# Probabilities for the memory rows: turned on 64 columns and copied into blocks, and fill that does not stop at a tile's end

## The chip, the cores and the metric

The kernel runs on one NeuronCore of a Trainium2 chip. The metric is the time of one execution on the device, in microseconds (us). An execution that was profiled gives, besides its time, a record of every instruction on every engine: TensorE (PE, and PEld for its weight loads), VectorE (DVE), ScalarE (ACT), GpSimd (POOL) and SyncE (SP, which issues most of the DMA transfers). In all profile lines here, Lnnn is line nnn of the kernel before.

## The reference

A layer norm, an attention with a recurrent memory, a residual, a second layer norm and a feed-forward block, on 2048 tokens of 640 numbers. The attention has 32 heads of 128. It goes through the tokens in 64 segments of 32, and 8 memory rows are put in front of each segment:

```python
for s in range(n_seg):
    h = concatenate([mem, x[s]])            # 8 + 32 rows
    q, k, v = h @ Wq, h @ Wk, h @ Wv        # 32 heads x 128
    p = softmax(where(mask, q @ k.T * scale, -1e9))   # memory rows see all 40, tokens are causal
    o = (p @ v) @ Wo
    mem = o[:8]                             # memory of the next segment
    out[s] = o[8:]
h = x + out
y = h + relu(layernorm(h) @ w1 + b1) ** 2 @ w2 + b2
```

The memory rows make it a chain: the projections of segment s + 1 need the eight output rows of segment s.

## The kernel before, in words

**Steps.** `step(b, sp)` does one segment; 16 blocks b of 128 tokens have four segments each, 64 steps in all. Weights stay in SBUF. A step projects q, k and v of 32 rows: the 8 memory rows and the segment's first 24 tokens. The last 8 tokens of each segment ("tails") need no memory, so their projections are done for many segments at once, as fill. Each projection has two halves n = 0, 1 of 16 heads: five chunks of the model dimension times four column groups, 20 matmuls of 512 columns.

**The memory rows' softmax** is done ahead of the tokens', in two halves of 16 heads. `scores(n)` (L494) makes a tile sm in which partition 32g + 8j + m holds memory row m of the head numbered 4g + j in that half, over 40 keys. `soft1(n)` (L500 to L505) takes the maximum mx on DVE and the exponential em with its sum zm on ACT. `soft2a(n)` (L510 to L519) takes 1/zm into rm (L512), spreads the 8 tail keys into four blocks of 8 columns with the 0/1 mask `same` (L514), and makes pm (L516): the 64 columns of em, four times over, each copy times rm and times `own`, a 128x4 mask that is 1 for the g-th copy in the partitions of group g alone. `soft3` (L523) turns pm, 128x256, in blocks of 32x32 on DVE. The result pT holds, for group g, the turned probabilities of that group in its own 32 partitions and zeros in the others; so that one matmul per head group can take v's 128 partitions against it (`values(n)`, L526 to L537: 16 matmuls L531 and 4 L536). `values_out(n)` copies the result into oT, half 0 on ACT (L245), half 1 on DVE (L243).

**The order around it** is written by hand; each engine runs its instructions in the order of the program, and waits are added where data or buffers need them. After the second half of k the order on PE is: `scores(0)`, v's first half (px, L233; out by ACT L589), the first chunk of v's second half, `scores(1)`, the rest of v's second half (ps; out by ACT L609), the tokens' own scores (L581, tile sk), fill, `values(0)`, fill, `values(1)`, then the 64 matmuls with wo (pw, L269). On DVE: mx(0), kT, rm(0), L514, pm(0), mx(1), the first half's turn, rm(1), L514, pm(1), the second half's turn, the causal mask (L611), oT, and the tokens' softmax (L640 to L651). Behind wo come the rest of the fill and `token_values` of the step before, while ACT (L284, L285) and DVE (L286, L379) bring the eight new memory rows into hT, on which the next step's q projection waits. POOL spreads q into qz (L440, L442), copies tails into qT and kT (L388, L384) and scales the tokens' probabilities (L653, L656).

**Fill** is a list of units, each one chunk of a tail projection (4 matmuls) or a tenth of a tail's wo (4 or 8 matmuls of 320 columns), of which `portion` gives some 8 to a step. `run(q, n, held, stop)` runs n of them. The unit that ends a tile returns its evacuation; this is put into `held` and done by `settle` later, behind `values(1)`, or for wo behind the tokens' tk. With `stop` true, `run` ends there:

```python
            ahead = 0 if ready else max(1, len(fill) // 2)
            run(fill, ahead // 2, held, True)
            values(0, pT0, po[1][0])
            values_out(0, po[1][0])
            run(fill, ahead - ahead // 2, held, True)
            values(1, pT1, po[1][1])
```

**Buffers.** The PSUM pool `mm` has three tiles for the halves of q, k and v, for sk and for the fill. em has one buffer for both halves; pT had two. pm shares a buffer with the tokens' pk.

Of the kernel before, what the change touches and what calls it, by code (L numbers as in the profile page):

```python
# [9 lines left out]
ALU = mybir.AluOpType  # L10
AX = mybir.AxisListType
F32 = mybir.dt.float32
BF16 = mybir.dt.bfloat16
# [3 lines left out]
def kernel(  # L17
# [31 lines left out]
    TL = SEG - HD  # L49
# [12 lines left out]
    const = ctx.enter_context(tc.tile_pool(name="const", bufs=1))  # L62
# [6 lines left out]
    s1 = ctx.enter_context(tc.tile_pool(name="s1", bufs=1))  # L69
    s2 = ctx.enter_context(tc.tile_pool(name="s2", bufs=2))  # L70
# [20 lines left out]
    for g in range(G):  # L91
        r = slice(32 * g, 32 * g + 32)
        nc.vector.tensor_copy(out=same[r], in_=ident[r, r].rearrange("p (j k) -> p j k", k=TL))
    nc.vector.tensor_reduce(out=diag[:], in_=same[:], op=ALU.add, axis=AX.X)
    nc.vector.tensor_copy(out=same[:], in_=diag[:].unsqueeze(2).to_broadcast([128, 4, TL]))
    own = const.tile([128, G], BF16)
    qT = const.tile([128, H, SEG], BF16)
    CW = 5 * SEG
    hTs = [const.tile([128, DC * CW], BF16, name="hT%d" % k) for k in range(2)]
# [40 lines left out]
    for q in range(4):  # L140
        nc.vector.tensor_copy(out=o0[32 * q:32 * q + 32, :].rearrange("m (c f) -> m c f", f=32),
                              in_=mem0[:].rearrange("m (c q f) -> m q c f", q=4, f=32)[:, q])
# [92 lines left out]
    def mmtile():  # L235
        return mm.tile([128, 512], F32, tag="mm", name="ps")
# [54 lines left out]
    fill, late, mid, nook = [], [], [], []  # L291

    def run(q, n, held=None, stop=False):
        while n > 0 and q:
            out = q.pop(0)()
            if out and held is not None:
                held.append(out)
                if stop:
                    break
            elif out:  # L300
                out[1]()
            n -= 1
# [148 lines left out]
    def step(b, sp, v=None):  # L451
        s = b * 4 + sp
        last = s == NS - 1
        lhs = rows_of(b, sp)
        ready = v is not None
# [31 lines left out]
        sms, ems, zms = {}, {}, {}  # L487

        def scores(n):
            sm = chn.tile([128, 512], F32, tag="ch", name="sm")  # L490
            for j in range(4):
                for g in range(G):
                    p = n * 16 + g * 4 + j
                    nc.tensor.matmul(sm[32 * g:32 * g + 32, 0:NK], lhsT=qz[:, p, :], rhs=kT[:, p, :],  # L494
                                     start=(j == 0), stop=(j == 3), skip_group_check=True)
            sms[n] = sm

        def soft1(n):
            mx = s2.tile([128, 1], F32, tag="mx", name="mx")
            nc.vector.tensor_reduce(out=mx[:], in_=sms[n][:, 0:NK], op=ALU.max, axis=AX.X, negate=True)  # L500
            em = s2.tile([128, SEG + NK], BF16, tag="em", name="em", bufs=1)
            zm = s2.tile([128, 1], F32, tag="zm", name="zm")
            nc.scalar.activation(out=em[:, SEG:], in_=sms[n][:, 0:NK], func=ACT.Exp, bias=mx[:, 0:1], scale=1.0,  # L503
                                 accum_out=zm[:])
            ems[n], zms[n] = em, zm  # L505

        def soft2(n):
            return soft3(soft2a(n))

        def soft2a(n):  # L510
            rm = s2.tile([128, 1], F32, tag="rm", name="rm")
            nc.vector.reciprocal(out=rm[:], in_=zms[n][:])  # L512
            pm = s1.tile([128, HG, 32], BF16, tag="pk", name="pm")[:].rearrange("p (g a) k -> p g (a k)", g=G)
            nc.vector.tensor_tensor(out=ems[n][:, 0:SEG].rearrange("p (j k) -> p j k", k=TL),  # L514
                                    in0=ems[n][:, 2 * SEG:].unsqueeze(1).to_broadcast([128, 4, TL]), in1=same[:], op=ALU.mult)
            nc.vector.scalar_tensor_tensor(out=pm, in0=ems[n][:, 0:2 * SEG].unsqueeze(1).to_broadcast([128, G, 2 * SEG]),  # L516
                                           scalar=rm[:, 0:1], in1=own[:].unsqueeze(2).to_broadcast([128, G, 2 * SEG]),
                                           op0=ALU.mult, op1=ALU.mult)
            return pm  # L519

        def soft3(pm):
            pT = s2.tile([128, G, 2 * SEG], BF16, tag="pTm", name="pTm")
            nc.vector.transpose(out=pT[:], in_=pm)  # L523
            return pT

        def values(n, pT, po):  # L526
            cols = po[:, 0, 0:128]
            for j in range(4):
                i = n * 4 + j
                for k in range(4):  # L530
                    nc.tensor.matmul(cols[32 * k:32 * k + 32].rearrange("p (g i m) -> p i g m", g=G, i=4)[:, j],  # L531
                                     lhsT=v[:, i * E + 32 * k:i * E + 32 * k + 32],
                                     rhs=pT[:, :, SEG + j * M:SEG + (j + 1) * M],
                                     start=(j == 0), stop=False, skip_group_check=True)
            for k in range(4):
                nc.tensor.matmul(cols[32 * k:32 * k + 32].rearrange("p (g a) -> p g a", g=G), lhsT=vt4[:, sp, n, 32 * k:32 * k + 32], rhs=pT[:, :, 0:SEG],  # L536
                                 start=False, stop=True, skip_group_check=True)  # L537

        def values_out(n, po):
# [23 lines left out]
        vt4 = vt4s[b]  # L563
# [13 lines left out]
        def token_scores(n):  # L577
            skv = view()
            for j in range(4):
                for g in range(G):  # L580
                    nc.tensor.matmul(skv[32 * g:32 * g + 32, n * 4 + j, :], lhsT=qT[:, n * 16 + g * 4 + j, :],  # L581
                                     rhs=kT[:, n * 16 + g * 4 + j, :], start=True, stop=True,
                                     skip_group_check=True)
# [6 lines left out]
            ps1 = mmtile()  # L590
            proj(wv, "half", lhs, 1, ps1, 0, 1)
        if not last:
            pm0 = soft2a(0)
            scores(1)
            soft1(1)
            pT0 = soft3(pm0)
# [6 lines left out]
        if not last:  # L603
            sk = mmtile()
            token_scores(0)
            token_scores(1)
            pT1 = soft2(1)
        if not ready:
            nc.scalar.copy(out=v[:, 512:1024], in_=ps1[:])  # L609
        def causal(skv):  # L610
            nc.vector.tensor_tensor(out=skv[:, :, M:NK], in0=skv[:, :, M:NK],  # L611
                                    in1=mask[:].unsqueeze(1).to_broadcast([128, HG, SEG]), op=ALU.add)

        held = []
# [4 lines left out]
        po = po_tiles()  # L619
        if last:  # L620
            run(fill, max(1, (len(fill) - 3) // 2), held, True)
            token_values(s - 1, *prevs[-2], po)
            token_out(s - 1, po)
            settle(held, True)
            run(fill, 2, held)
            settle(held, True)
            causal(skv)
        else:
            ahead = 0 if ready else max(1, len(fill) // 2)
            run(fill, ahead // 2, held, True)  # L630
            values(0, pT0, po[1][0])
            values_out(0, po[1][0])
            run(fill, ahead - ahead // 2, held, True)
            values(1, pT1, po[1][1])
            causal(skv)
            values_out(1, po[1][1])
            settle(held, True)
# [14 lines left out]
        pkt = s1.tile([128, HG, TL], BF16, tag="pkt", name="pkt")  # L652
        nc.gpsimd.tensor_tensor(out=pkt[:], in0=ek[:, :, SEG:NK], in1=rk[:].unsqueeze(2).to_broadcast([128, HG, TL]),  # L653
                                op=ALU.mult)
        pk = s1.tile([128, HG, 32], BF16, tag="pk", name="pk")
# [3 lines left out]
        if not last:  # L659
# [10 lines left out]
            held = []  # L670
# [10 lines left out]
        pTt = s1.tile([128, 2, 32], BF16, tag="pTt", name="pTt")  # L681
# [105 lines left out]
    def start():  # L787
# [45 lines left out]
        for n in range(2):  # L833
# [31 lines left out]
    nc.gpsimd.memset(mask[0:TL], 0.0)  # L865
    nc.gpsimd.affine_select(out=mask[0:TL], in_=mask[0:TL], compare_op=ALU.is_ge, fill=NEG, base=HD,
                            pattern=[[-1, SEG]], channel_multiplier=1)
    nc.gpsimd.memset(own[:], 0.0)
    for g in range(G):
        nc.gpsimd.memset(own[32 * g:32 * g + 32, g:g + 1], 1.0)  # L870
# [4 lines left out]
    for b in range(2, NB):  # L875
        for which in "qk":
            u = tail_units(b, which)
            plan += [(4 * b - 3 + (which == "k"), 4 * b - 5, u[DC * n:DC * n + DC]) for n in range(2)]
    for b in range(10, NB):
        u = tail_units(b, "v")  # L880
# [81 lines left out]
    for t in range(S // NT):  # L962
# [8 lines left out]
        for fc in range(FC):  # L971
            ps = mmtile()
            for c in range(DC):
# [43 lines left out]
        for q in range(NK4):  # L1017
# [6 lines left out]
            for hh in range(2):  # L1024
                k = pr + 2 * hh
# [44 lines left out]
```

## Time and profile before

| | us |
|---|---|
| runs of the kernel | 966.51, 966.9, 968.98; median 966.9 |
| the profiled execution | 965.13 |
| its span, first to last instruction | 963.0 |
| PE busy | 930.4 (97%) |
| DVE, ACT, POOL busy | 711.7, 538.5, 280.7 |
| steps 1 to 62, each | 12.2 |
| L516, pm, 126 times | 61.1, 485 ns each |
| L523, the turn of pm, 126 times | 56.0, 445 ns each |
| granted clock of TensorE | 0.998 |

Busy time of PE counts an instruction from start to end, and matmuls overlap in it. The chain of waits follows the work that ended last back from step to step: what stands in it had nothing to hide behind, and what does not stand in it was beside other work. In the timeline a row is a start, a duration, the engine, the line, the operation, the tiles and the shapes, and how often.

### The profile page before, as it was taken

The page shows a single profiled execution, that of the slowest core. Times are in us where ns is not written, and L with a number is a line of the kernel's source. Part 1 is how long each engine was busy: PE and PEld are TensorE (multiplying, and loading weights), DVE is VectorE, ACT ScalarE, POOL GpSimd, SP SyncE. Part 2 cuts the span into 40 slices and gives each one's busy share as a digit, 9 for nine tenths or more (in the row PEclk, how much of TensorE's full clock was granted, in tenths as well). Part 3 has the DMA queues.
Part 4 walks back from the last instruction along what each step waited for, and adds up shares of the span by engine and source line. Part 5 has one row for each costly group of instructions (what it writes and reads, how often), then busy time and mean ns, then how long its engine had stood idle before and what let it go on. Part 6 is the DMA issues. An engine that isn't in the chain of part 4 may idle for free.

```text
span 963.0 us, 55579 instructions
## 1 busy us (share of the span) xinstructions
PE 930.4 (97%) x24749; PEld 556.5 (58%) x24760; DVE 711.7 (74%) x2068; ACT 538.5 (56%) x1397; POOL 280.7 (29%) x875
## 2 busy tenths in 40 slices
PE   6979999999999999999999999999999999999998
PEld 2445566556565656556565656556655565555555
DVE  5178888778877787887878787878887788656532
ACT  2546666566666566666666566656665665523321
POOL 2113323232323222322232223232323233254300
PEclk9999999999999999999999999999999999999999
DMA  9972201010101001110101010101010220543320
GB/s 354 402 254 69 39 17 28 14 29 14 23 19 27 17 18 27 20 25 9 32 14 31 12 32 12 33 13 33 6 34 6 54 42 21 190 119 82 97 55 28
DMA packets 65872, 56.63 MB, mean 59 GB/s; under 512 B 37384, under 2 KB 61712, under 8 KB 63712
## 3 DMA queue, kind: packets, MB, share of 16 engines
q1 hardware_dynamic: 65392, 52.74, 19.3%
q8 instruction: 194, 3.18, 1.4%
q14 instruction: 46, 0.38, 0.1%
q0 software_dynamic: 224, 0.33, 0.1%
q10 hardware_dynamic: 16, 0.01, 0.0%
HBM read 38.37 MB, written 9.44 MB: 50 GB/s over the span
## 4 chain that ended last, share of the span: by engine, by line
PE 70%; DVE 17%; ACT 5%; DMA 4%; issue 2%; SPq 2%; ACTq 0%; POOL 0%; DVEq 0%
PE ps L233 19%; PE pw L269 15%; PE px L233 9%; PE pk L233 7%; PE y L1027 6%; PE ps L975 6%; DVE pm L516 5%; DVE kT L484 4%; DVE pTm L523 2%; PE ps L269 2%; ACT em L503 2%; DMA wq<-in_A_Wq_dram 2%; PE po L420 2%; PE po L531 2%; SPq L150 2%
## 5 line engine op out<-in xcount | busy, mean ns | idle before, releaser
L233 PEld LDWEIGHTS <-hT 128*32 128x32 bf16 x7680 | 190.8, 96 | 175.0 <-DVE hT L379 15.8
L269 PE MATMUL pw<-wo,oT 128*32 128x320 bf16 x4224 | 159.7, 299 | 4.3 <-issue 1.9
L269 PEld LDWEIGHTS <-oT 128*32 128x32 bf16 x4224 | 119.7, 96 | 26.7 <-issue 7.8
L257 DVE STREAM_TRANSPOSE qT<-row 128x512 bf16<-128x512 bf16 x128 | 89.5, 699 | 42.7 <-ACT row L252 42.5
L653 POOL TENSOR_TENSOR pkt<-ek,rk 128x64 bf16<-128x64 bf16 x64 | 18.9, 295 | 286.1 <-ACT otmp L285 213.7
L233 PE MATMUL ps<-wv,hT 128*32 128x512 bf16 x1260 | 89.5, 378 | 0.0
L647 ACT ACTIVATE ek<-tk 128x320 bf16<-128x320 f32 x64 | 30.1, 470 | 100.6 <-DVE tk L642 99.5
L233 PE MATMUL ps<-wq,hT 128*32 128x512 bf16 x1260 | 81.2, 382 | 3.2 <-DVE hT L379 3.0
L233 PE MATMUL ps<-wk,hT 128*32 128x512 bf16 x1280 | 80.5, 379 | 0.0
L233 PE MATMUL px<-wq,hT 128*32 128x512 bf16 x1260 | 79.4, 379 | 0.0
L233 PE MATMUL px<-wv,hT 128*32 128x512 bf16 x1260 | 79.2, 378 | 0.0
L233 PE MATMUL pk<-wk,hT 128*32 128x512 bf16 x1240 | 78.2, 379 | 0.0
L431 ACT CAST oT<-po 128x512 bf16<-128x512 f32 x128 | 68.7, 589 | 15.1 <-PE po L425 12.5
L983 ACT ACTIVATE wv<-ps,b1f 128x512 bf16<-128x512 f32 (+1 forms) x56 | 37.6, 672 | 66.6 <-PE ps L975 65.6
L233 PEld LDWEIGHTS <-hTt 128*32 128x32 bf16 x1920 | 53.1, 97 | 29.6 <-issue 4.7
L440 POOL COPY qz<-qT 128x96 bf16<-128x96 bf16 x126 | 33.4, 265 | 109.5 <-DVE qT L257 109.5
L516 DVE SCALAR_TENSOR_TENSOR pm<-em,rm,own 128x256 bf16<-128x256 bf16 x126 | 61.1, 485 | 4.6
L284 ACT COPY otmp<-pw 64x96 f32<-64x96 f32 (+2 forms) x129 | 28.9, 224 | 58.0 <-PE pw L269 36.9
L1027 PE MATMUL y<-wq,wk 128*128 128x320 bf16 x416 | 58.9, 299 | 0.2
L252 ACT ACTIVATE row<-ps 128x512 bf16<-128x512 f32 x93 | 54.7, 611 | 5.5 <-PE ps L233 4.7
L523 DVE STREAM_TRANSPOSE pTm<-pm 128x256 bf16<-128x256 bf16 x126 | 56.0, 445 | 2.2
L481 ACT CAST row<-ps 128x256 bf16<-128x256 f32 x126 | 40.8, 375 | 29.6 <-PE ps L233 29.6
(132 smaller groups left out, 1801.4 us busy)
## 6 DMA issues: line engine op xcount, KB each, us to landing
wv<-in_A_Wv_dram SPq DMA_DIRECT2D x5, 1024.0 KB
wq<-in_A_Wq_dram SPq DMA_DIRECT2D x5, 1024.0 KB
wk<-in_A_Wk_dram SPq DMA_DIRECT2D x5, 1024.0 KB
wo<-in_A_Wo_dram SPq DMA_DIRECT2D x8, 640.0 KB
o_all<-o SPq DMA_DIRECT2D x256, 7.5 KB
vt<-vt_d SPq DMA_DIRECT2D x60, 64.0 KB
xt<-in_A_x_dram SPq DMA_DIRECT2D x19, 160.0 KB
wq<-in_B_w_dram SPq DMA_DIRECT2D x1, 2080.0 KB
```

What stands on the lines that cost most here:

```text
L233: nc.tensor.matmul(ps[32 * k:32 * k + 32, :], lhsT=lhs(c), rhs=wr[:, c, n, k], start=(c == 0), stop=(c == DC - 1))
L252: nc.scalar.mul(out=row, in_=ps, mul=scale)
L257: nc.vector.transpose(out=dst[:, n * 16:(n + 1) * 16, 0:32], in_=row.rearrange("p (h e) -> p h e", e=32))
L269: nc.tensor.matmul(pw[32 * j:32 * j + 32, c0:c0 + DH], lhsT=lhs(p), rhs=wov2[:, head(p), ch], start=(h == 0), stop=(h == 15))
L431: nc.scalar.copy(out=oTg[:, gs, :, :, 0:SEG], in_=po[1][h][:, :, 0:256].rearrange("p g (n j q) -> p g n j q", n=2, q=32))
L481: nc.scalar.copy(out=row[:, u * 256:(u + 1) * 256], in_=ps[:, u * 256:(u + 1) * 256])
L484: nc.vector.transpose(out=dst[:, n * 16 + u * 8:n * 16 + u * 8 + 8, 0:32], in_=row[:, u * 256:(u + 1) * 256].rearrange("p (h e) -> p h e", ...
L516: nc.vector.scalar_tensor_tensor(out=pm, in0=ems[n][:, 0:2 * SEG].unsqueeze(1).to_broadcast([128, G, 2 * SEG]), scalar=rm[:, 0:1], in1=own ...
L523: nc.vector.transpose(out=pT[:], in_=pm)
L975: nc.tensor.matmul(ps[:], lhsT=w1[:, c, fc * 128:(fc + 1) * 128], rhs=hnT[:, c, :], start=(c == 0), stop=(c == DC - 1))
L983: nc.scalar.activation(out=r[:, 0:w], in_=ps[:, 0:w], func=ACT.Relu, bias=b1f[:, fc:fc + 1], scale=1.0)
L1027: nc.tensor.matmul(y[hh][:, 0:DH], lhsT=f1T[:, fc, k * 128:(k + 1) * 128], rhs=w2[:, fc, cs], start=(fc == 0 and not hf), stop=(fc == FFUL ...
```

## The change

For the first half of the heads the probabilities are no longer spread over 256 columns before the turn. `soft2(0)` multiplies em's 64 columns by rm into a 128x64 pm (in the buffer of the tokens' pkt). `soft3` turns these 64 columns (into the buffer of the tokens' pTt) and copies the four groups of 32 partitions, 32x64 each, into their blocks of a constant tile pBs[0]: group 0 on DVE, 1 on ACT, 2 and 3 on POOL. The rest of pBs[0] is set to zero once, on POOL, at the start. The second half is made as before, in pBs[1], which has one buffer now. ACT's copy of v's second half (L609) stands ahead of `soft2(1)` in the program; ACT's and DVE's own orders are not changed by that. For the fill, `ahead` is rounded up and `stop` is no longer given, so that a run goes on into the next tile when one ends; the evacuations still wait in `held`.

```diff
+    pBs = [const.tile([128, G, 2 * SEG], BF16, name="pB%d" % k) for k in range(2)]
...
         def soft2(n):
-            return soft3(soft2a(n))
-
-        def soft2a(n):
             rm = s2.tile([128, 1], F32, tag="rm", name="rm")
             nc.vector.reciprocal(out=rm[:], in_=zms[n][:])
-            pm = s1.tile([128, HG, 32], BF16, tag="pk", name="pm")[:].rearrange("p (g a) k -> p g (a k)", g=G)
             nc.vector.tensor_tensor(out=ems[n][:, 0:SEG].rearrange("p (j k) -> p j k", k=TL),
                                     in0=ems[n][:, 2 * SEG:].unsqueeze(1).to_broadcast([128, 4, TL]), in1=same[:], op=ALU.mult)
+            if n == 0:
+                pm = s1.tile([128, HG, TL], BF16, tag="pkt", name="pm")[:].rearrange("p i k -> p (i k)")
+                nc.vector.tensor_scalar(out=pm, in0=ems[n][:, 0:2 * SEG], scalar1=rm[:, 0:1], scalar2=None, op0=ALU.mult)
+                return pm
+            pm = s1.tile([128, HG, 32], BF16, tag="pk", name="pm")[:].rearrange("p (g a) k -> p g (a k)", g=G)
             nc.vector.scalar_tensor_tensor(out=pm, in0=ems[n][:, 0:2 * SEG].unsqueeze(1).to_broadcast([128, G, 2 * SEG]),
                                            scalar=rm[:, 0:1], in1=own[:].unsqueeze(2).to_broadcast([128, G, 2 * SEG]),
                                            op0=ALU.mult, op1=ALU.mult)
-            return pm
+            nc.vector.transpose(out=pBs[1][:], in_=pm)
+            return pBs[1]
 
         def soft3(pm):
-            pT = s2.tile([128, G, 2 * SEG], BF16, tag="pTm", name="pTm")
-            nc.vector.transpose(out=pT[:], in_=pm)
-            return pT
+            pT = s1.tile([128, 2, 32], BF16, tag="pTt", name="pT")[:].rearrange("p u k -> p (u k)")
+            nc.vector.transpose(out=pT, in_=pm)
+            for g, copy in enumerate((nc.vector.tensor_copy, nc.scalar.copy, nc.gpsimd.tensor_copy, nc.gpsimd.tensor_copy)):
+                r = slice(32 * g, 32 * g + 32)
+                copy(out=pBs[0][r, g], in_=pT[r])
+            return pBs[0]
...
-            pT1 = soft2(1)
         if not ready:
             nc.scalar.copy(out=v[:, 512:1024], in_=ps1[:])
+        if not last:
+            pT1 = soft2(1)
...
-            ahead = 0 if ready else max(1, len(fill) // 2)
-            run(fill, ahead // 2, held, True)
+            ahead = 0 if ready else (len(fill) + 1) // 2
+            run(fill, ahead // 2, held)
             values(0, pT0, po[1][0])
             values_out(0, po[1][0])
-            run(fill, ahead - ahead // 2, held, True)
+            run(fill, ahead - ahead // 2, held)
             values(1, pT1, po[1][1])
...
+    nc.gpsimd.memset(pBs[0][:], 0.0)
     nc.gpsimd.memset(own[:], 0.0)
```

More of the change, by code (lines that the diff above doesn't have):

```diff
@@ L518, in soft2a, with values @@
                                            op0=ALU.mult, op1=ALU.mult)
-            return pm
+            nc.vector.transpose(out=pBs[1][:], in_=pm)
+            return pBs[1]
         def soft3(pm):
-            pT = s2.tile([128, G, 2 * SEG], BF16, tag="pTm", name="pTm")
-            nc.vector.transpose(out=pT[:], in_=pm)
-            return pT
-        def values(n, pT, po):
+            pT = s1.tile([128, 2, 32], BF16, tag="pTt", name="pT")[:].rearrange("p u k -> p (u k)")
[4 more added lines that the diff above has]
+            return pBs[0]
+        def values(n, pB, po):
             cols = po[:, 0, 0:128]
@@ L532, in values @@
                                      lhsT=v[:, i * E + 32 * k:i * E + 32 * k + 32],
-                                     rhs=pT[:, :, SEG + j * M:SEG + (j + 1) * M],
+                                     rhs=pB[:, :, SEG + j * M:SEG + (j + 1) * M],
                                      start=(j == 0), stop=False, skip_group_check=True)
             for k in range(4):
-                nc.tensor.matmul(cols[32 * k:32 * k + 32].rearrange("p (g a) -> p g a", g=G), lhsT=vt4[:, sp, n, 32 * k:32 * k + 32], rhs=pT[:, :, 0:SEG],
+                nc.tensor.matmul(cols[32 * k:32 * k + 32].rearrange("p (g a) -> p g a", g=G), lhsT=vt4[:, sp, n, 32 * k:32 * k + 32], rhs=pB[:, :, 0:SEG],
                                  start=False, stop=True, skip_group_check=True)
@@ L592, in step @@
         if not last:
-            pm0 = soft2a(0)
+            pm0 = soft2(0)
             scores(1)
```

## The prediction

> **What bounds the kernel now.** I read the page first, then the waits, then the chain of waits and the timeline of one step.
>
> ```profile
> PE 930.4 (97%) x24749; PEld 556.5 (58%) x24760; DVE 711.7 (74%) x2068; ACT 538.5 (56%) x1397; POOL 280.7 (29%) x875
> ...
> PE 70%; DVE 17%; ACT 5%; DMA 4%; issue 2%; SPq 2%; ACTq 0%; POOL 0%; DVEq 0%
> ```
>
> PE looks full, yet 17% of the chain that ended last lies on DVE: somewhere in each step PE waits for vector work and has only fill to cover it. The chain of waits in step 35 (the 62 steps from step 1 to step 62 take 12.2 us each) shows where:
>
> ```profile
> 484.48 0.48 DVE pm L516
> 484.97 0.12 DVE mx L500
> ...
> 485.17 0.40 ACT em L503 x2
> ...
> 485.59 0.16 DVE rm L512
> 485.76 0.08 DVE em L514
> ...
> 485.86 0.50 DVE pm L516
> ...
> 486.38 0.46 DVE pTm L523
> 486.84 0.04 issue
> 486.88 0.27 PE po L531 x16
> ```
>
> The first half's pm stands in front of the second half's maximum (mx); from there one line runs through em, rm, em, pm and pTm to the second half's values (po L531). The timeline of the same stretch, with the PE rows:
>
> ```profile
> 484.32 0.33 PE L494 MATMUL sm<-kT,qz 128*32 128x40 bf16 x16
> ...
> 485.56 0.59 ACT L609 CAST v<-ps 128x512 bf16<-128x512 f32 x1
> ...
> 486.16 0.59 PE L269 MATMUL ps<-wo,oTt 128*32 128x320 bf16 x12
> ...
> 486.88 0.27 PE L531 MATMUL po<-pTm,v 128*32 128x32 bf16 x16
> ```
>
> Call Z the end of the second half's scores, 484.32 + 0.33 = 484.65. values(1) starts at Z + 2.23. Reading the same two events in all 62 steps, 57 have 2.22 to 2.23, whatever fill lies between: this time is set by the chain, not by PE. PE would be there sooner. Matmuls overlap, so I count by starts: a fill unit of four 512-wide matmuls takes 0.216 us (20 of them start at 481.85, the next group at 482.93), a 320-wide one 0.0339 (64 in 2.17). With two units ahead of each values, PE would reach values(1) at Z + 1.96. Summed over the steps, PE stands 19.4 us there: all that this edit can win at this place. Behind the last wo matmul the next q projection starts 1.48 us later whether no fill or four 512-wide units lie between, and 1.69 with five: four units just cover the way of the memory rows (wo, otmp, o, hT), and a fifth costs 0.17 with the tail of the projection counted.
>
> **The change, part by part.**
>
> Chain. pm(0) falls from 128x256 with two SBUF inputs (485 ns) to 128x64 with one. No row has that shape; above it is the 128x640 tensor_scalar (L192, 434 ns), below it the 128x32 tensor_tensor (155 ns). I take 0.15. pm(0) ends at 484.63, so mx(1) now waits for Z. A DVE instruction starts 0.05 after a PE result (po L536 ends 487.22, oT L243 starts 487.27): mx(1) at 484.70 instead of 484.89, 0.20 long when it does not start inside another's end, em(1) 0.1 later at 485.00 instead of 485.17. ACT is free (v L589 ends 484.92). Gain 0.17, at most 0.19. Between, DVE does the 128x64 transpose (row pTt L682: 207 ns, some 0.14 behind mx) to 485.04 and one 32x64 copy, about 0.1, to 485.18: done before rm(1), which follows em(1) by 0.42, at 485.42. DVE is freed of some 0.4 us a step in all, which nothing waits for.
>
> Copies. ACT's comes behind em(1)'s accumulator read (ends 485.39): a 64x64 copy is 204 ns (L285), the 128x320 exp from SBUF 470 (L647), so 0.20 to 0.26, until 485.64. Behind it in ACT's queue is v (L609), at 485.56 before: 0.05 to 0.07 later. POOL sits idle here (its last, L388, ends 484.32): 128x32 copies are 210, 128x96 are 265, so a pair is 0.24 + 0.18. A POOL copy follows a DVE result by 0.07 (481.63 to 481.70): 485.11 to 485.53, or to 485.60 if DVE's copy holds it back. So pB[0] is whole at about Z + 1.05. values(0) starts at Z + 1.37 with two units ahead, and Z + 0.98 with none (steps 60 and 62, where the chain, not PE, leads): the three new waits on PE are covered, with 0.3 us of margin in most steps.
>
> One thing speaks against this. Where a POOL instruction reads SBUF, a DVE tensor_tensor with two SBUF inputs waits for it:
>
> ```profile
> 52.74 0.54 POOL L388 COPY qT<-qTt 128x128 bf16<-128x128 bf16 x2
> ...
> 53.05 0.25 DVE L514 TENSOR_TENSOR em<-em,same 128x32 bf16<-128x32 bf16 x1
> 53.42 0.48 DVE L516 SCALAR_TENSOR_TENSOR pm<-em,rm,own 128x256 bf16<-128x256 bf16 x1
> ```
>
> L514 takes 0.156 elsewhere and pm follows 0.19 behind its start; here L514 takes 0.254, ends 0.02 after POOL's copies (53.28), and pm starts 0.14 after them. In the last stage the 128x512 tensor_tensor L984, 426 ns alone, takes 1417 beside POOL's L770 (876.64). [...] In the chain, pm(1) would start at 485.69 without a wait (0.27 behind rm(1)), and 0.14 after POOL's end at 485.67 to 485.74: I charge 0.02 (0 to 0.05). values(1) goes to Z + 2.08, a gain of 0.15.
>
> Fill. ahead is rounded up and no longer ends at a tile's end. I counted both kernels' matmuls slot by slot. In 34 steps nothing moves: they gain 34 x 0.15 = 5.0 (in one, PE is the bound and gives 0.05). In 19 steps one or two units move from behind wo to ahead of the values. The later part gains 3.4 in all (mostly 0.17, from five units to four); values(1) is held by PE at Z + 2.17 where a third unit lies there (8 steps) and by the chain elsewhere, gaining 1.8: together 5.2. In nine steps (4, 7, 15, 23, 26, 34, 42, 45, 53) a tile ends ahead of values(0) and the next now begins there too. Of the three mm buffers one holds sk, one the finished tile, whose evacuation still comes after values(1), and one v's second half until L609 is done. The trace shows the price: in these nine the new tile, then behind values(0), starts at Z + 1.55, 0.06 after L609's end (Z + 1.49), with PE waiting up to 0.23. Now values(0) stands behind it: start Z + 1.62, values(0) about Z + 1.83, values(1) about Z + 2.43, 0.2 later than before, given back by 0.17 to 0.4 behind wo: +0.3 in all.
>
> Setup. One POOL memset and the SP queue's order (one wo tail's four writes ahead of an x load and a transpose, both due steps later): nothing.
>
> Sum: -5.0 - 5.2 + 0.3 = -9.9. Against the profiled execution, 965.1 (span 963.0 and 2.1 around it), 955.2. The median of the runs shown is 1.8 above it, so 966.9 - 9.9 = **957.0 us**. With mx at its earliest and no port wait: -11.4; and were the nine steps free of their buffer wait too: -15.2, 951.7.
>
> **Rivals.**
>
> *The chain gain is eaten on DVE.* POOL's pair starts before DVE's own copy, which waits until both are done: 485.60, its end 485.70, rm(1) near 485.66 instead of 485.59, values(1) no earlier than now. Only the fill is left: -3.1, or +0.5 if the whole 0.07 counts; 963.8 to 967.4. [...] Against: DVE follows itself in 0.04 (pm ends 486.34, pTm starts 486.38), POOL in 0.07. This is also the time if the chain does not shorten for another reason.
>
> *Slower: POOL's pair lasts too long.* It decides when L514 of the second half may run, and values(0) as well. With the 0.14 behind POOL's end, a pair of about 0.66 us (end 485.77, pm(1) 485.91 instead of 485.86) eats what the fill gives; beyond that, each 0.1 costs some 5 us. At 0.43 a copy, the row of the 256-wide kT L384, the pair ends at 485.97, pm(1) starts at 486.11, values(1) at Z + 2.48: +10.7, 977.6. For it: the copies have a form POOL does not run now (32 partitions). Against: its narrow copies all lie between 0.20 and 0.27.
>
> *values(0) waits for a late quarter*, ACT's above all: no cost up to Z + 1.4; at Z + 1.62 PE becomes the bound nearly everywhere and -1.5 is left, 965.4. Against: ACT's queue is empty between em(1) and v.
>
> **How the numbers follow.** Forecast 0.62 (-6 to -15 around -10); chain eaten 0.15; POOL too long 0.15; late quarter 0.08. About 0.3%, 2.9 us, can be told from no change. The forecast and a small part of the first rival are faster: 0.65; the first and third rivals mostly the same: 0.19; the second slower: 0.16. The range runs from the lower bound, 952, to the first rival's upper end, 967.5; it leaves out the slower case and little else.
>
> **What would show it.** Right: mx(1) starts 0.05 after its scores; values(1) at Z + 2.05 to 2.12 in the 34 untouched steps; in the nine steps PE idles before values(0); 4 units behind wo nearly everywhere; POOL's pair near 0.45. Wrong: L514 of the second half, or DVE's quarter copy, well over 0.16 us long; PE idle before values(0) with releaser POOL or ACT in ordinary steps; L609 later than Z + 1.0.

## The result and the profile after

| | before | after |
|---|---|---|
| median of the runs, us | 966.9 (965.38 to 968.98, 5 runs) | 961.71 (960.89 to 961.93, 5 runs) |
| profiled execution, us | 965.13 | 961.72 |
| its span, us | 963.0 | 959.9 |

The ratio is 0.994, 95% interval 0.9924 to 0.9956: 5.2 us faster, where the prediction said 9.9 faster (957.0, range 952 to 967.5). The direction held; the size was about half.

From here on, lines of the changed kernel have its own numbers: the second half's scores are L495 (before L494), mx L501, em L504, rm L510, the spread of the tail keys L511, pm(0) L515, pm(1) L518, the turn of pm(1) L521, the turn of pm(0) L526, the four copies L529, values L537 and L542, v's second half L614, the projections L234, wo L270. The page's lines of engines and of the chain's shares, after:

```profile
PE 927.6 (97%) x24749; PEld 554.5 (58%) x24760; DVE 701.8 (73%) x2131; ACT 555.2 (58%) x1460; POOL 312.3 (33%) x1002
...
PE 87%; DMA 5%; DVE 3%; ACT 2%; SPq 2%; issue 1%; POOL 0%; ACTq 0%; DVEq 0%
```

DVE's share of the chain fell from 17% to 3%, and PE's rose from 70% to 87%. The chain follows one path only: two paths that end close together, in step 35 the turn of pm(1) at 484.77 and the fill's ps at 484.79, can change places in it. Its part in step 35 shows that here; columns are start, duration, what:

```profile
482.52 0.16 PE sm L495 x16
...
484.38 0.41 PE ps L270 x12
...
484.82 0.28 PE po L537 x16
```

No DVE row is left in this step: the chain now runs through PE, from the scores to the second half's values. The timeline says how close DVE still is:

```profile
482.35 0.33 PE L495 MATMUL sm<-kT,qz 128*32 128x40 bf16 x16
...
482.51 0.24 DVE L515 TENSOR_SCALAR pm<-em,rm 128x64 bf16<-128x64 bf16 x1
482.75 0.20 DVE L501 TENSOR_REDUCE mx<-sm 128x1 f32<-128x40 f32 x1
...
483.04 0.29 ACT L504 ACTIVATE em<-sm,mx 128x40 bf16<-128x40 f32 x1
...
483.23 0.51 POOL L529 COPY pB<-pT 32x64 bf16<-32x64 bf16 x2 [0.89 <-DVE pT L526]
...
483.54 0.23 DVE L511 TENSOR_TENSOR em<-em,same 128x32 bf16<-128x32 bf16 x1
...
483.72 0.59 ACT L614 CAST v<-ps 128x512 bf16<-128x512 f32 x1
483.80 0.48 DVE L518 SCALAR_TENSOR_TENSOR pm<-em,rm,own 128x256 bf16<-128x256 bf16 x1
...
484.32 0.45 DVE L521 STREAM_TRANSPOSE pB<-pm 128x256 bf16<-128x256 bf16 x1
```

Z, the end of the scores, is 482.35 + 0.33 = 482.68. The maximum starts at Z + 0.07 (before 0.24) and em at Z + 0.36 (before 0.52): 0.16 gained. But L511 is 0.23 long instead of 0.156; it ends at 483.77, 0.03 behind POOL's two copies (483.23 + 0.51). So pm(1) starts at Z + 1.12, before 1.21, the turn ends at 484.77, and values(1) starts at 484.82 = Z + 2.14: of the 0.16, 0.09 arrive.

Over the 62 steps the trace after has two kinds. In 29 of them L511 takes 0.155 and values(1) comes at Z + 2.06 in the median; in 33 it takes 0.23, and the median is Z + 2.14. Where L511 is long, POOL's second copy took 0.237; where L511 is short, the copy took 0.289 to 0.295 in 27 of the 29 steps. A step of the short kind, step 33:

```profile
459.08 0.56 POOL L529 COPY pB<-pT 32x64 bf16<-32x64 bf16 x2 [0.89 <-DVE pT L526]
...
459.38 0.15 DVE L511 TENSOR_TENSOR em<-em,same 128x32 bf16<-128x32 bf16 x1
```

So either can hold the other off, L511 by 0.08 or the copy by 0.05. Which one came first does not show in the recorded starts: L511 starts at Z + 0.86, and POOL's second copy 0.03 ahead of it, in both kinds (in 60 of the 62 steps).

In the nine steps where a new tile begins ahead of values(0), PE waits for the buffer; PE and ACT in step 34:

```profile
471.45 0.59 ACT L614 CAST v<-ps 128x512 bf16<-128x512 f32 x1
...
472.09 0.40 PE L234 MATMUL ps<-wv,hTt 128*32 128x512 bf16 x4 [0.32 <-ACT v L614]
...
472.31 0.28 PE L537 MATMUL po<-pB,v 128*32 128x32 bf16 x16
...
472.89 0.28 PE L537 MATMUL po<-pB,v 128*32 128x32 bf16 x16
```

The tile waits 0.32 for L614, which itself starts 0.13 later against the scores than before (Z + 1.04 in step 35, before 0.91), because ACT's copy lies ahead of it. In this step, and in most of the nine, values(0) comes at Z + 1.88 and values(1) at Z + 2.47.

Set against the steps of the prediction, steps 1 to 61 of the two traces differ by (us):

| part | predicted | measured |
|---|---|---|
| steps in which no fill moved (33) | -5.0 | -3.7 |
| steps with moved fill (19) | -5.2 | -1.5 |
| of these: up to values(1); behind wo; between values(1) and the last wo matmul | -1.8; -3.4; 0 | -2.1; -2.8; +3.4 |
| steps with the buffer wait (9) | +0.3 | +1.1 |
| sum | -9.9 | -4.1 |
| ahead of step 1 and behind the attention | 0 | +1.0 |

The last two rows make -3.1, the difference of the two profiled spans. The medians differ by more, 5.2, because the profiled execution of before was 1.8 under its median.

One entry is as large as any gain and was not in the sum at all: +3.4 between values(1) and the last of the 64 wo matmuls, where the change edits nothing. In the trace after PE stands there in some steps and waits for nothing that the profile names; step 61, which had no such stand before:

```profile
800.72 0.26 PE L537 MATMUL po<-pB,v 128*32 128x32 bf16 x12
...
801.89 0.20 PE L537 MATMUL po<-pB,v 128*32 128x32 bf16 x4 [0.91 <-issue]
```

Twelve matmuls of values(1), then 0.91 us of nothing, then the other four. I numbered PE's instructions (matmuls, weight loads and the 182 waits and drains that the trace has of its queue, in the order of their starts) and looked at where such stands fall. All twelve stands of steps 1 to 62 that make a matmul start over 0.4 us behind the one before, with no wait named, lie at numbers that leave 193 or 194 when divided by 256. The queue of instruction transfers has the same spacing (queue, kind: transfers, MB, share):

```profile
q8 instruction: 194, 3.18, 1.4%
```

194 transfers of 16 KB, for the page's 24,749 + 24,760 = 49,509 matmuls and weight loads and those 182: one for each 256. Each stand ends 2.2 to 2.8 us after one of these transfers began (the transfer itself takes 0.9 to 1.5 us). So the theory was: PE's instructions come in blocks of 256, a block can be used some 2.2 us or more after its transfer starts, and where a border between blocks falls into wo or values, where PE starts a matmul every 0.034 us (wo, 64 in 2.17) or 0.008 (values, 20 in 0.16), PE gets there sooner and stands.

### The profile page after: what moved, and what is told of

Read it like the earlier page. It is cut to its first block, busy times and chain, and to the rows that moved or that the text cites. A ratio compares the mean times of both kernels' runs of the same rounds, so it can differ in the third digit from the quotient of the medians.

```text
span 959.9 us, 55964 instructions
## 1 busy us (share of the span) xinstructions
PE 927.6 (97%) x24749; PEld 554.5 (58%) x24760; DVE 701.8 (73%) x2131; ACT 555.2 (58%) x1460; POOL 312.3 (33%) x1002
## 4 chain that ended last, share of the span: by engine, by line
PE 87%; DMA 5%; DVE 3%; ACT 2%; SPq 2%; issue 1%; POOL 0%; ACTq 0%; DVEq 0%
PE ps L234 28%; PE pw L270 15%; PE px L234 13%; PE pk L234 7%; PE y L1035 6%; PE ps L983 6%; PE ps L270 3%; DMA wq<-in_A_Wq_dram 2%; PE po L421 2%; SPq L151 2%; PE po L537 2%; PE sm L495 1%; PE ps L587 1%; DMA wo<-in_A_Wo_dram 1%; PE po L542 1%
## 5 line engine op out<-in xcount | busy, mean ns | idle before, releaser
L234 PEld LDWEIGHTS <-hT 128*32 128x32 bf16 x7680 | 187.3, 96 | 179.4 <-DVE hT L380 23.0
L270 PE MATMUL pw<-wo,oT 128*32 128x320 bf16 x4224 | 160.5, 299 | 5.7 <-issue 3.3
L270 PEld LDWEIGHTS <-oT 128*32 128x32 bf16 x4224 | 120.2, 96 | 27.7 <-issue 9.4
L234 PE MATMUL ps<-wv,hT 128*32 128x512 bf16 x1260 | 89.4, 378 | 0.0
L234 PE MATMUL ps<-wq,hT 128*32 128x512 bf16 x1260 | 81.6, 383 | 3.3 <-DVE hT L380 2.8
L234 PE MATMUL ps<-wk,hT 128*32 128x512 bf16 x1280 | 80.3, 379 | 0.0
L234 PE MATMUL px<-wq,hT 128*32 128x512 bf16 x1260 | 79.2, 379 | 0.0
L234 PE MATMUL px<-wv,hT 128*32 128x512 bf16 x1260 | 79.0, 378 | 0.0
L234 PE MATMUL pk<-wk,hT 128*32 128x512 bf16 x1240 | 77.9, 379 | 0.0
L234 PEld LDWEIGHTS <-hTt 128*32 128x32 bf16 x1920 | 53.3, 97 | 32.3 <-issue 8.7
L253 ACT ACTIVATE row<-px 128x512 bf16<-128x512 f32 x63 | 37.6, 597 | 32.2 <-PE px L234 32.2
L287 DVE TENSOR_TENSOR o<-pw,otmp 128x96 bf16<-128x96 f32 (+2 forms) x129 | 31.4, 243 | 31.5 <-ACT otmp L286 25.9
```

What stands on the lines that cost most here:

```text
L234: nc.tensor.matmul(ps[32 * k:32 * k + 32, :], lhsT=lhs(c), rhs=wr[:, c, n, k], start=(c == 0), stop=(c == DC - 1))
L253: nc.scalar.mul(out=row, in_=ps, mul=scale)
L270: nc.tensor.matmul(pw[32 * j:32 * j + 32, c0:c0 + DH], lhsT=lhs(p), rhs=wov2[:, head(p), ch], start=(h == 0), stop=(h == 15))
L287: nc.vector.tensor_tensor(out=five(o[:])[:, cs], in0=blocks(0, 128, 32)[:, cs], in1=five(tmp[:])[:, cs], op=ALU.add)
```

## The experiments

Each was timed with the kernel before on the same chip. "Stand" is the time between values(1) and the last wo matmul beyond 2.21 us, summed over steps 1 to 62 of the profiled execution. The kernel before gave 964.16 to 967.68 in these groups, so ratios are compared, and times only inside a group. The expectations give times beside the first 966.9, so a time can miss its range where the ratio keeps it (e2, e4), or the other way round (e1, e3).

| run | us (median) | before | ratio, 95% interval | stand |
|---|---|---|---|---|
| before | | 966.9 | | 6.3 |
| after | 961.71 | 966.9 | 0.994 (0.9924 to 0.9956) | 9.7 |
| e1_chain_alone | 960.02 | 964.16 | 0.9964 (0.995 to 0.9977) | 8.0 |
| e2_fill_alone | 961.83 | 964.16 | 0.9975 (0.996 to 0.9989) | 6.1 |
| e3_one_pool | 959.76 | 964.16 | 0.9953 (0.9934 to 0.9972) | 5.9 |
| e4_stop_first | 957.54 | 964.16 | 0.9933 (0.9914 to 0.9952) | 6.9 |
| after_again | 959.41 | 965.9 | 0.9937 (0.9916 to 0.9958) | 9.9 |
| e6_shift | 956.59 | 965.9 | 0.9908 (0.9891 to 0.9925) | 6.9 |
| e7_pool_twice (one run) | 981.77 | 965.9 | | |
| e8_direct | 970.22 | 965.9 | 1.0046 (1.003 to 1.0061) | 4.7 |
| e9_before_shift | 967.91 | 967.68 | 1.0003 (0.999 to 1.0017) | 5.4 |
| e10_stop_shift | 957.78 | 967.68 | 0.9908 (0.9887 to 0.9929) | 8.0 |
| e11_act_two | 960.46 | 967.68 | 0.9926 (0.9907 to 0.9945) | 6.3 |
| e12_shift_whole | 959.76 | 965.28 | 0.9944 (0.9925 to 0.9964) | 8.3 |

**The two halves of the change, each alone.** e1_chain_alone has the new softmax and the old fill:

```diff
-            ahead = 0 if ready else (len(fill) + 1) // 2
-            run(fill, ahead // 2, held)
+            ahead = 0 if ready else max(1, len(fill) // 2)
+            run(fill, ahead // 2, held, True)
...
-            run(fill, ahead - ahead // 2, held)
+            run(fill, ahead - ahead // 2, held, True)
```

> The new first half (64 columns, four copies) with the old fill. Theory: the chain is worth most of the gain, values(1) comes 2.06 or 2.14 us behind the second half's scores instead of 2.23, which is 62 steps x some 0.12 = 7.4 us, less up to 3 us of PE standing without a wait at the ends of its 256-instruction blocks: 959.5 to 963. Rival: the chain's gain is given back elsewhere and the fill made the difference: 965.5 or more.

e2_fill_alone is the kernel before with the edits of `ahead` and `run` alone.

> The old softmax with the new fill. Theory: the units moved are worth 2.8 us by the counted slots, and in nine steps values(0) waits for a buffer until 1.83 us behind the scores; with the standing at instruction blocks free to go either way by 2 us: 962 to 967, within 0.3% of before or little better. Rival (the fill is the gain): 962 or less.

Measured: 0.9964 and 0.9975, 4.1 and 2.3 us under the same kernel before. Both parts win, and they add: 0.36% and 0.25% against 0.6% for both. For e2 the theory expected within 0.3% of before, which holds; its 961.83 us is just what its rival asked for, in a group whose before was 2.7 lower. e2's trace has values(1) at Z + 2.22 in 48 of 62 steps, as before the change, and at Z + 2.35 to 2.37 in eight: the fill does not touch the chain. The chain's part is smaller than the sums of the prediction, with values(1) at Z + 2.06 in 13 steps of e1 and at Z + 2.13 or 2.14 in 40.

**Is it POOL that holds L511?** e3_one_pool lets DVE make two of the copies and POOL one ("shared port" in the expectations is a name for this hold; no run shows what it is made of):

```diff
-            for g, copy in enumerate((nc.vector.tensor_copy, nc.scalar.copy, nc.gpsimd.tensor_copy, nc.gpsimd.tensor_copy)):
+            for g, copy in enumerate((nc.vector.tensor_copy, nc.scalar.copy, nc.vector.tensor_copy, nc.gpsimd.tensor_copy)):
```

> The changed kernel with the third quarter copied by DVE, so that POOL copies one. Theory (shared port): POOL is done before the second half's tensor_tensor em,same; that row is 0.156 us in every step instead of up to 0.23, and values(1) comes 2.06 us behind the scores wherever PE does not hold it, not 2.14: 1.5 us less than the changed kernel, 960.2, 959 to 961.5. Rival (the late pm has to do with DVE's own order): the row stays at 0.23 and the time at 961.7 or, with another copy ahead of rm, above it.

```profile
494.93 0.37 DVE L529 COPY pB<-pT 32x64 bf16<-32x64 bf16 x2
...
495.03 0.23 POOL L529 COPY pB<-pT 32x64 bf16<-32x64 bf16 x1 [0.95 <-DVE pT L526]
...
495.33 0.16 DVE L510 RECIPROCAL rm<-zm 128x1 f32<-128x1 f32 x1
...
495.41 0.15 DVE L511 TENSOR_TENSOR em<-em,same 128x32 bf16<-128x32 bf16 x1
```

L511 is 0.155 in 61 of 62 steps: with POOL done early the long form is gone, so POOL's second copy was the cause. The time doesn't gain by it (0.9953 against 0.994, the intervals overlap), because the second DVE copy ends at 495.30 and rm starts at 495.33, 0.50 behind em's start instead of 0.42: the 0.08 is paid in another place, and values(1) is at Z + 2.14 again. Also seen: DVE's two copies (494.93 to 495.30) and POOL's (495.03 to 495.26) ran side by side at about their usual lengths (0.17 and 0.23 each), so neither held the other off here.

**What a longer POOL pair costs.** e7_pool_twice makes each POOL copy twice:

```diff
                 copy(out=pBs[0][r, g], in_=pT[r])
+                if g > 1:
+                    copy(out=pBs[0][r, g], in_=pT[r])
```

> The changed kernel with each of POOL's two copies made twice, the same data to the same place. Shared port: the second half's tensor_tensor em,same waits for the end of four copies, about 0.5 us more, pm behind it too; values(1) comes 0.45 us or more later in every step: 25 to 30 us, 987 to 992. Rival (POOL only delays values(0) through pB): em,same stays below 0.25 us, values(0) starts near 1.6 us behind the scores, values(1) at 2.2: 3 to 6 us, 965 to 968.

Its lines from the copies on have numbers higher by 2 (values(0) is L539):

```profile
496.33 0.48 DVE L518 SCALAR_TENSOR_TENSOR pm<-em,rm,own 128x256 bf16<-128x256 bf16 x1
496.44 0.48 POOL L529 COPY pB<-pT 32x64 bf16<-32x64 bf16 x1
...
497.26 0.28 PE L539 MATMUL po<-pB,v 128*32 128x32 bf16 x16 [0.44 <-POOL pB L531]
```

981.77: about 16 us over before, and neither expectation has the way it came about. L511 stayed at 0.156 beside the second of the four copies; then pm(1), two SBUF inputs, started 0.11 ahead of the third, and this copy took 0.48 instead of 0.23. The last copy ended at 497.21, and values(0) waited 0.44 for it. So POOL's copies can last too long, as the slower rival has it, but the hold goes both ways, and what it hits first is values(0), not pm(1).

**Without copies on the way.** e8_direct has DVE turn groups 0 and 1 straight into pBs[0] and groups 2 and 3 together, which leaves one copy each to ACT and POOL (with the stop of e4, below; its lines keep the numbers of after):

```diff
-            nc.vector.transpose(out=pT, in_=pm)
-            for g, copy in enumerate((nc.vector.tensor_copy, nc.scalar.copy, nc.gpsimd.tensor_copy, nc.gpsimd.tensor_copy)):
+            nc.vector.transpose(out=pT[64:128], in_=pm[64:128])
+            for g, copy in ((3, nc.gpsimd.tensor_copy), (2, nc.scalar.copy), (0, nc.vector.transpose), (1, nc.vector.transpose)):
                 r = slice(32 * g, 32 * g + 32)
-                copy(out=pBs[0][r, g], in_=pT[r])
+                copy(out=pBs[0][r, g], in_=pT[r] if g > 1 else pm[r])
```

> The fill of the run that stops ahead of values(0) only, and the first half's quarters otherwise: DVE turns quarters 0 and 1 straight into their blocks, without copies, after it has turned 2 and 3 together, of which ACT copies one and POOL one. Theory (shared port): POOL has one copy and is done before em,same; that row is 0.156 us everywhere, rm is not late as it was with two DVE copies, values(1) comes 2.06 us behind the scores in the untouched steps: 2 us under the run with the stop alone, ratio to before 0.991. Rival: three DVE instructions in place of two push rm back and values(1) is at 2.14 or later: 0.993 or more.

```profile
499.87 0.24 DVE L526 STREAM_TRANSPOSE pT<-pm 64x64 bf16<-64x64 bf16 x1
499.93 0.29 ACT L504 ACTIVATE em<-sm,mx 128x40 bf16<-128x40 f32 x1
...
500.14 0.48 DVE L529 STREAM_TRANSPOSE pB<-pm 32x64 bf16<-32x64 bf16 x2
...
500.65 0.17 DVE L510 RECIPROCAL rm<-zm 128x1 f32<-128x1 f32 x1
```

Slower than before, 1.0046, by the way of the rival. Turning 64 columns takes 0.24 here on 64 or 32 partitions as it does on 128 in after, so three turns fill DVE until 500.62. rm(1) starts 0.72 behind em instead of 0.42, and values(1) moves from Z + 2.22 to Z + 2.36 or 2.37 in 57 of 62 steps. L511 is 0.156 in all steps, and that is worth nothing beside it.

**The stop ahead of values(0).** e4_stop_first gives the stop at a tile's end back to the first `run` alone:

```diff
-            run(fill, ahead // 2, held)
+            run(fill, ahead // 2, held, True)
```

> The changed kernel with the fill ahead of values(0) stopping at a tile's end again; behind values(0) it goes on. Theory (buffer): in steps 4, 7, 15, 23, 26, 34, 42, 45 and 53 the new tile waits for its buffer behind values(0) and values(1) comes at 2.3 us or sooner behind the scores instead of 2.47: 1.6 us less by the slots, 960.1, 959 to 961.5. Rival: what is lost there is all given back behind wo: 961.7.

0.9933: not to be told from the change itself in time. Its trace shows what it does: in the nine steps the time up to values(1) is 2.9 us shorter in all, 1.6 of these are given back behind wo, and 0.4 more is gained in front of the fill: 1.8 us better there. As a measured time that size is below what these runs resolve.

**The stands.** after_again is the changed kernel once more, beside e6_shift, which has 128 PE instructions (64 transposes of a constant) in front, and nothing else:

```diff
+    pad = mm.tile([128, 1024], BF16, tag="mm", name="pad")
+    for k in range(64):
+        nc.tensor.transpose(out=pad[:, k % 8 * 128:k % 8 * 128 + 128], in_=ident[:], identity=ident[:])
```

> The changed kernel once more, as the measure for the runs beside it on this chip. Every theory: ratio to before 0.994, within 0.002.

> The changed kernel with 64 transposes of the identity, 128 PE instructions, put in front of everything, where PE waits for its first data anyway. Theory (instruction supply): PE's standing without a wait sits where its instruction count reaches 193 or 194 modulo 256, so by 128 more instructions every such place moves within the step: steps 8, 31, 32, 40, 48, 55, 56, 57, 59 and 61 are free of it at the old instruction and others have it, and its sum changes by some us either way, the time with it, 961.7 with 3 on either side. Rival (the steps have it because of their transfers or their fill): the same steps stand at the same instructions, and the time is 961.7.

More work, and 2.8 us less time in the median: 956.59 against 959.41; the intervals of the two ratios just overlap. The time lies below the range expected (961.7, 3 on either side). The stands between values(1) and the last wo matmul leave steps 1, 8, 31, 32, 39, 40, 47, 48, 55, 56, 57 and 61 (0.25 to 1.10 us each in after) and come up in 12, 13, 20, 28, 35, 36, 43, 44, 51 and 52 (0.34 to 0.75), at 193 to 195 modulo 256 as before. In the 19 steps with moved fill the stretch loses 2.8 us, the greater part of the +3.4 of the table above.

The control, e9_before_shift, puts the same three lines into the kernel before:

> The kernel before with 128 PE instructions (64 transposes of a constant) put in front, and nothing else changed. Theory (PE stands where it crosses into a 16 KB block of its instructions sooner than some 2.2 us after that block's transfer began, so a shift moves the blocks' borders to other places of the steps): the stands inside values and wo leave steps 31, 39, 40, 48, 55 and 56 and appear in others, their sum falls or rises by a few us from 6.3, and the time goes with it: 962 to 969, no direction forecast. Rival (the 64 transposes help any kernel, for instance because something at the start comes off better): the steps keep their stands and the time falls by some 3 us as it did for the changed kernel, 963.

1.0003: there the shift is worth nothing. Its stands move as well (31, 39, 40, 48, 55, 56 are free; 12, 20, 28, 35, 36, 44, 52 and 59 have 0.3 to 0.9), but their sum was low to begin with and stays so, 5.4 for 6.3. And e12_shift_whole has 128 transposes, 256 instructions, one whole block:

> The changed kernel with 256 PE instructions in front (128 transposes of a constant), twice what the shift by half a block had: one whole block of 16 KB. Theory (where PE stands inside values and wo is set by the place of the blocks' borders): a whole block brings every border back to where it was in the changed kernel, so the stands return to steps 1, 8, 16, 31, 32, 39, 40, 47, 48, 56 and 61, leave steps 12, 13, 20, 28, 35, 36, 43, 44, 51 and 52, sum up to 9 to 10.5 us again, and the time is that of the changed kernel, ratio 0.9935 to 0.9955. Rival (what helped was PE work at the front as such, or the start that it moves): steps 12, 20, 28, 35, 44, 51, 52 keep their stands or there are none, and the time is that of the shift by half a block or less, ratio 0.991 or lower.

The stands are back where the changed kernel had them (steps 1, 8, 17, 24, 31, 39, 40, 47, 48, 55, 56, 61), gone from 12, 13, 20, 28, 35, 36, 43, 44, 51 and 52, the instruction transfers are 195 instead of 194, and the ratio is 0.9944, that of the change. Their sum, 8.3, is less than the 9 to 10.5 that I expected; single stands differ by some tenths between executions. Steps 16 and 32, which I had named too, stayed short. PE work at the front as such, the rival, is out: with twice as much of it the gain is gone.

How long PE stands at a border is another matter. e3 has the changed kernel's PE program, with the borders at the same matmuls. In its step 61 PE stands at the same place as in after, for 0.22 instead of 0.91:

```profile
800.95 0.20 PE L537 MATMUL po<-pB,v 128*32 128x32 bf16 x4 [0.22 <-issue]
```

Over the 19 steps with moved fill, the stretch behind values(1) is longer than before by 3.4 us in after, 2.3 in after_again, 1.9 in e12 and 1.4 in e3, all with the same borders; by 1.9 in e2 (new fill, old chain), 0.8 in e1 (old fill) and 0.6 in e6. These are single executions, and that of after_again (964.27) was 4.9 over its median. So 3.4 is the largest of four executions with the same borders.

**Both remedies, and one more for L511.** e10_stop_shift is e4 with the shift of 128; e11_act_two is that with two copies on ACT:

```diff
-            for g, copy in enumerate((nc.vector.tensor_copy, nc.scalar.copy, nc.gpsimd.tensor_copy, nc.gpsimd.tensor_copy)):
+            for g, copy in enumerate((nc.vector.tensor_copy, nc.scalar.copy, nc.scalar.copy, nc.gpsimd.tensor_copy)):
```

> The changed kernel with the stop at a tile's end given back ahead of the first half's values, and with the same 128 PE instructions in front. Theory: the two gains are of different kinds (buffer wait in nine steps; borders of instruction blocks), but the stop alone had a stand of 6.9 us in values and wo where the changed kernel had 9.8, so of the shift's 3 us most is had already: 954.5 to 957.5 against 957.5 without the shift. Rival (the shift is worth 3 us whatever the stands): 954.

> The same, and of the four copies DVE makes one, ACT two and POOL one. Theory (the second half's em multiplication is held by POOL's pair, by 0.08 us in half the steps): with one POOL copy, over well ahead, that multiplication takes 0.156 in all steps, and the second half's values come 2.24 after the last of its scores starts in nearly all chain steps (now 2.31 to 2.36 in some 30 of 61): -2.4. Against it: ACT's eviction of v's second half comes 0.24 later, at about 1.7 after the scores' start, and a fill tile that waits for its buffer begins 0.24 later in up to nine steps: +0.5 to +1.5. Net 1 to 2 us under the kernel with the stop and the shift alone. Rival (the last quarter, now on ACT some 1.4 after the scores' start, becomes what the first half's values wait for): values(0) has ACT as releaser in most steps, and the time is no better or some us worse.

e10: 0.9908, the same as e6; 957.78 lies just above the range expected, 954.5 to 957.5, on a chip whose kernel before was slower too (967.68). The stop and the shift do not add up to a time that can be told from the shift alone, and here the shift did not shorten the stands (8.0, for 6.9 in e4).

e11 missed: 0.9926, 2.7 us behind e10, with overlapping intervals. L511 is 0.154 in all 62 steps, as the theory has it, and values(1) is at Z + 2.06 in 20 steps, twice as many as in e10. But (lines higher by 3: copies L532, v's second half L617, values L540):

```profile
480.60 0.49 ACT L532 COPY pB<-pT 32x64 bf16<-32x64 bf16 x2
...
481.12 0.59 ACT L617 CAST v<-ps 128x512 bf16<-128x512 f32 x1
...
481.76 0.31 PEld L540 LDWEIGHTS <-v 128*32 128x32 bf16 x16 [0.16 <-ACT v L617]
```

L617 is v's second half, the values' own input. It is done 0.24 later, at 481.71, and in 15 steps values(1) waits for it and comes at Z + 2.35. The rival's mechanism shows as well: 45 times the weight loads of values(0) wait for an ACT copy, 11.0 us in all. I had counted the later L617 only against the fill's buffers, and not against the matmuls that read v.

## Why the prediction was half right

**What bounds the kernel, and what the chain gains.** Right. The first half's pm stood in front of mx(1); made shorter, mx(1) starts at Z + 0.07 (predicted 0.05) and em gains 0.16 (0.17), and e1 alone is faster. pm(0) takes 0.24 where I took 0.15 and ends at 482.75, just where mx(1) starts; that can be the 0.02 by which mx(1) is late, and no more.

**"I charge 0.02 (0 to 0.05)" for the wait behind POOL's pair** is a term that was mis-sized. That POOL's copies hold a DVE multiplication of two SBUF inputs (0.254 for 0.156 in the rows of before), and the place, were right; that it is a port ("no port wait" in the sum) no run shows, only the lengthening. Measured are 0 in 29 steps and 0.08 in 33. Two lengths made it: POOL's pair starts 0.13 behind the turn, not 0.07, and takes 0.51, not 0.42 (0.56 where L511 is short), so it ends where L511 should, and not ahead of it. That is most of what the 33 untouched steps lack, 3.7 instead of 5.0; e3 and e11, with one POOL copy, show that POOL's second copy is the cause. Two signs named for being wrong came with it: L511 well over 0.16, and L614 (L609 before) later than Z + 1.0.

**The nine steps with the buffer wait: "+0.3 in all"**, measured +1.1. The order of events was right. L614 stands 0.13 later, not 0.07, and values(0) comes at Z + 1.88 instead of 1.83 and values(1) at 2.47 instead of 2.43; seven steps with about 0.04 too much are 0.3 of the 0.8. Nearly all the rest lies in steps 4 and 53, where values(1) comes at Z + 2.69 and 2.75. What is given back behind wo is as counted.

**"The later part gains 3.4 in all ... together 5.2"** is the step that failed most. Its two terms held: -2.1 for -1.8 up to values(1), and -2.8 for -3.4 behind wo. What failed is the silent premise that the stretch between them keeps its length. It grew by 3.4 us in these steps, because PE stands there at the borders of its own instruction blocks, a cost that the sum put at nothing. e6, e9 and e12 show that the place of the stands goes by the borders: they move with half a block and come back with a whole one. It is not that the change lays more borders there: counted by number, 15 of the 19 steps have one in the stretch before and 16 after (41 and 42 of all 62), moved by up to 16 instructions. The stands at them are longer. e2 and e1 point to the moved fill (1.9 with it, 0.8 without); but 1.4 to 3.4 with the same borders says that most of the size is open.

**Rivals.** The first (the gain eaten on DVE) did not come about as told: DVE's own copy starts at 483.14, 0.09 ahead of POOL's, and rm follows em by 0.42 as before. That DVE's copy waits for POOL's, or POOL's pair for DVE's copy (485.60 in both cases), was the author's supposition: no run shows it, and in e3 such copies ran side by side at 0.17 and 0.23. Half of the gain was eaten all the same in half of the steps, one instruction later, at L511. The second (POOL's pair too long) did not decide here; e7 shows that it does when the pair is twice as long, by way of values(0). The late quarter on ACT is covered with one copy and not with two (e11).

**Open.** The 1.0 us ahead of step 1 and behind the attention lies within what those parts differ by between the profiles of other kernels here (the stretch from step 62 to the end takes 147.1 to 148.6 us). What sets the moment at which a block's transfer starts, and so how long a stand gets, was not found. The numbering does not cover every stand either: after_again has two of 0.86 and 0.74 us between the starts of two matmuls of the tokens' own scores, at 122 and 138 modulo 256, and e3 and e11 have one each.

## What to carry to other kernels

When a wait of 0.15 us per step is to be won, price the copies that replace it on the engine that they can hold off (L511 0.23 us for 0.155 here): between hidden and charged lay some tens of ns, and each way of taking POOL's part off (DVE, ACT, more turns) moved the price to the next instruction in that engine's queue. Ask of every eviction that a new instruction delays who reads it, not only which buffer it frees. And where a profile has PE waiting for "issue" in a dense stretch, number PE's instructions modulo 256 before the stand is put down to the edit: with 128 instructions of nothing at the front this change took 2.8 us less in the median, at the edge of what the runs resolve, and the kernel before no less at all. One execution is not enough to size such stands: four executions with the same borders gave 1.4 to 3.4 us for the same 19 steps.

## What the runs showed of the hardware

- PE's stands without a named wait, of over 0.4 us, came at one place modulo 256 instructions, counted with the queue's waits (193 to 195 in steps 1 to 62 of before, after and e6; after_again had two elsewhere), 2.2 to 2.9 us behind the start of a 16 KB instruction transfer of 0.9 to 1.5 us.
- L511 and pm(1), DVE instructions with two SBUF inputs, and POOL's copies held each other off, in both directions: L511 0.23 for 0.155 and a 32x64 POOL copy 0.291 for 0.237 beside L511 (after), and 0.48 for 0.23 beside pm(1) (e7). A DVE copy beside a POOL copy (e3) lengthened neither (0.17 and 0.23).
- Turning 64 columns on DVE took 0.24 us on 32, 64 (e8) and 128 partitions (after; 0.20 in most of the tokens' own turns there, L689); a 32x64 copy of SBUF took 0.17 on DVE, 0.24 on ACT, 0.23 on POOL (after).
